# RWKV5 attention and a SoLU feed-forward block on one core: where rows are centred, how the float64 weights become float32, in which order the first iterations run

## The chip, the core and the metric

The kernel runs on one core of a Trainium2 chip. The metric is the device time of one execution in microseconds (us), as the median of several runs. The engines are TensorE (PE; its weight loads are listed as PEld), VectorE (DVE), ScalarE (ACT), GpSimd (POOL) and SyncE (SP, which here only issues DMAs). Each works through its own queue in order.

## The reference

```python
# r, k, v: (4, 8, 768, 48) float32; w, u: (8, 48)
for t in range(S):
    cur = einsum('bhd,bhe->bhde', u[None] * kt, vt)
    y[:, :, t] = einsum('bhd,bhde->bhe', rt, state + cur)
    state = w[None, :, :, None] * state + einsum('bhd,bhe->bhde', kt, vt)
x = y.transpose(0, 2, 1, 3).reshape(3072, 384)
h = x @ w_in                                  # (384, 1024)
e = exp(h - max(h));  solu = h * e / (sum(e) + 1e-9)
ln = (solu - mean(solu)) / sqrt(var(solu) + 1e-6) * g_ln
out = ln @ w_out                              # (1024, 384)
```

The two weight matrices reach the kernel as float64 words, since the setup divides float32 by a float64 root; r, k, v, w, u and g_ln are float32.

## The kernel before

The 3072 rows are 24 units of 128 tokens (a batch element and a chunk of 128 steps). A main loop runs `i` from -2 to 30. In iteration `i` it transposes r and k of unit `i + 2` (`turn_r`, `turn_k`), computes the decayed scores of unit `i + 1` (`scores`, tile `at`, masked into `AT` by VectorE's `copy_predicated`), the attention output of unit `i` (`finish`: `y_ps`, copied to `xT`, and the state update `kv_ps`), the input product of unit `j = i - 2` (`ffn_in`: `h_ps = xT·w_in`, then `Exp` on ScalarE), the unnormalised SoLU of unit `j` (`unit`: tile `solu` and its statistics), and the transposes and output product of unit `l = i - 7` (`turn_ln`: `t_ps`, copied to `lnT`; `ffn_out`: `o_ps`). So iterations 2 to 6 are early ones: they have an input product and no output product yet. From `i = 7` on both stand in each iteration, until units run out.

The order on each engine is the order in which the Python code issues instructions (`manual_schedule`); tiles of a pool wait for the release of the tile that held the buffer before. `psH` is one buffer of two PSUM banks for `h_ps`, `psM` four single banks for everything that is tagged "m". At most eight of SP's DMAs are under way at a time: each waits for the eighth before it.

`kp` (k times decay) and `rku` (r·k·u, of which VectorE's `own` is the sum per head and `diagonal` the product with the identity on ScalarE) are made by GpSimd three units ahead.

Weights are converted in 14 pieces: 6 of `w_in` (128x512 words of 8 bytes) and 8 of `w_out` (128x384). Per piece, `convert_a` takes on ScalarE the magnitude of the high word read as float32 (`mag`) and the scaled low word (`low`), `convert_b` on VectorE clamps `mag` and builds the float32 bits from high word and `mag` (L524, L528, L530), `convert_c` on GpSimd adds the low part, and for `w_out` `convert_d` multiplies by g on ScalarE. One piece each is converted at `i = -2` and `-1`, two each at `i = 0` to `5`; `w_in` is complete after `i = 1`.

Layer norm's mean is taken out of the weights: `column_sums` (L651) accumulates the column sums of the converted `w_out` in a PSUM bank over iterations 3 to 6, `column_mean` makes them a mean on all partitions, and `centre` (L662) subtracts it from the eight blocks of `w_out`, four on VectorE and four on GpSimd, at the end of iteration 6. The variance then comes from the sum and the sum of squares of a row:

```python
nc.scalar.activation(out=X["e"], in_=solu, func=ACT.Square, accum_out=ss)
nc.gpsimd.tensor_mul(sqm, tot, tot)
nc.gpsimd.tensor_scalar(out=sqm, in0=sqm, scalar1=-1.0 / dff ** 2, scalar2=1e-6, ...)
nc.gpsimd.tensor_scalar(out=var, in0=ss, scalar1=1.0 / dff, scalar2=sqm, ...)
```

At the end `check_sums` tests the row sums and the decays; a flag then decides at run time whether a second, general path (`general_path`, unchanged) runs. It does not run on these inputs.

Of the kernel before, what the change touches and what calls it, by code (L numbers as in the profile page):

```python
# [9 lines left out]
F32 = mybir.dt.float32  # L10
# [386 lines left out]
def direct_path(  # L397
# [101 lines left out]

    def load_weights(j):  # L500
        dst, src, _ = pieces[j]
        raws[j] = wpool.tile([128, dst.shape[1], 2], U32, tag="raw", name="raw", bufs=5)
        nc.sync.dma_start(out=raws[j].rearrange("p n o -> p (n o)"), in_=src)


# [2 lines left out]
    def convert_a(j):  # L508
        raw = raws.pop(j)
        n = raw.shape[1]  # L510
        lo, hi = raw[:, :, 0], raw[:, :, 1]
        mag = wpool.tile([128, n], F32, tag="mag", name="mag", bufs=3)
# [4 lines left out]
        step[j] = hi, mag, low  # L517

    def convert_b(j):
        hi, mag, low = step[j]  # L520
        ma = wpool.tile([128, mag.shape[1]], U32, tag="ma", name="ma", bufs=4)
# [19 lines left out]
    def convert_d(j):  # L541
        dst, _, f = pieces[j]
        ma, low = step.pop(j)
        if f is not None:
            nc.scalar.activation(out=dst, in_=ma.bitcast(F32), func=ACT.Copy,
                                 scale=g_sb[:, f : f + 1])


    load(0, "kr")
    load_weights(0)  # L550
    load(1, "kr")
    load(0, "v")
    load_weights(1)
    load(1, "v")
    load_weights(2)
    load(2, "kr")
    load_weights(3)
    load(2, "v")
    load_weights(4)
    load(3)  # L560

    ident = const.tile([128, 128], F32, name="ident")
    make_identity(nc, ident)
# [61 lines left out]

    def check_sums():

        good = small.tile([128, N], F32, name="good", bufs=1)
        good2 = small.tile([128, N], F32, name="good2", bufs=1)
        low = small.tile([128, 1], F32, name="low", bufs=1)  # L630
        nc.vector.tensor_single_scalar(out=good, in_=sums, scalar=1.0 / MOST, op=ALU.is_ge)
        nc.vector.tensor_single_scalar(out=good2, in_=sums, scalar=MOST, op=ALU.is_le)
        nc.vector.tensor_mul(good, good, good2)
        nc.vector.tensor_reduce(out=low, in_=good, axis=AX.X, op=ALU.min)
        n_ps = psM.tile([1, 1], F32, tag="m", name="n_ps")
        nc.tensor.matmul(n_ps, low, part[:, 0:1], start=True, stop=True)
        nc.vector.tensor_scalar(out=bad, in0=n_ps, scalar1=all_ok, scalar2=127.5 / 32,
                                op0=ALU.mult, op1=ALU.is_lt)

    part = const.tile([128, 128], F32, name="part")
    mean_sb = const.tile([128, dm], F32, name="mean_sb")
    nc.gpsimd.memset(part, 1.0 / 32)
    mean = []

    def column_sums(fs):
        if fs and not mean:
            mean.append(psM.tile([128, dm], F32, tag="m", name="mean_ps"))
        for f in fs:  # L650
            nc.tensor.matmul(mean[0][ts(f % 4, 32), :], part[:, 0:32], w_out_sb[:, f, :],  # L651
                             start=(f < 4), stop=(f >= KF - 4), skip_group_check=True)
        if KF - 1 in fs:
            nc.scalar.copy(out=mean_sb, in_=mean[0])

    def column_mean():
        ps = psM.tile([128, dm], F32, tag="m", name="mean_ps2")
        nc.tensor.matmul(ps, part, mean_sb, start=True, stop=True)
        nc.scalar.activation(out=mean_sb, in_=ps, func=ACT.Copy, scale=32.0 / dff)  # L659

    def centre(f, engine):
        engine.tensor_sub(w_out_sb[:, f, :], w_out_sb[:, f, :], mean_sb)  # L662

    live = {}

# [107 lines left out]

    def ffn_in(i):
        X = live[i]
        h_ps = psH.tile([128, dff], F32, name="h_ps")
        for n in range(dff // NX):
            for j in range(KD):
                nc.tensor.matmul(h_ps[:, ts(n, NX)], X["xT"][:, j, :], w_in_sb[:, j, ts(n, NX)],  # L779
                                 start=(j == 0), stop=(j == KD - 1))  # L780
        e = X["e"] = fpool.tile([128, dff], F32, name="e")
        nc.scalar.activation(out=e, in_=h_ps, func=ACT.Exp, accum_out=sums[:, i : i + 1])  # L782
        X["h"] = h_ps

    def unit(i):
        X = live[i]
        st = small.tile([128, 8], F32, name="st", bufs=LO + 3)
        rs, tot, ss, sqm, var, rstd = (st[:, n : n + 1] for n in range(6))
# [12 lines left out]
        X["rstd"] = rstd  # L801
# [23 lines left out]
        nc.sync.dma_start(out=out[ds(b * S + c * T, T), :], in_=o)  # L825


    ahead = 5
    todo = list(range(len(pieces)))
    conversions = {-2: 1, -1: 1, 0: 2, 1: 2, 2: 2, 3: 2, 4: 2, 5: 2}  # L830
    now = []
    decay_k(0)
    for i in range(-2, N + LA + LO):
        j, l = i - LA, i - LA - LO
        if i == 0:
            nc.sync.dma_start(out=g_sb, in_=moe_g_ln.rearrange("(c p) -> p c", p=128))
        if 0 <= i and i + 4 < N:
            load(i + 4)
        if i + 2 < N:
# [5 lines left out]
        fs = [pieces[p][2] for p in now if pieces[p][2] is not None]  # L845
        for p in now:
            convert_d(p)
        now = [todo.pop(0) for _ in range(conversions.get(i, 0))]
        for n, p in enumerate(now):
            convert_a(p)  # L850
            if n == 0 or i < LA:
                convert_b(p)
            if ahead < len(pieces):
                load_weights(ahead)
                ahead += 1
        if i + 3 < N:
            decay_k(i + 3)
            if i < 0:
# [4 lines left out]
            weigh(i + 3, nc.gpsimd)  # L863
        if i == 10:
            check_range()
        if 0 <= l and not i > N + LA - 1:
            turn_ln(l)
        if 0 <= j < N:
            ffn_in(j)
        column_sums(fs)  # L870
        if i + 2 < N and l >= 0:
            diagonal(i + 2)
        if 0 <= l and 0 <= j < N:
            unit(j)
        if i >= N + LA - 1 and l + 1 < N:
            turn_ln(l + 1)
        if l == N - 1:
            check_sums()
        if 0 <= l:
            ffn_out(l)  # L880
        if 0 <= i + 1 < N:
            scores(i + 1)
        if 0 <= j < N and l < 0:
            unit(j)
        if i < 0:
            diagonal(i + 2)
        if 0 <= i < N:
            finish(i)
        if l < 0 <= i:
# [4 lines left out]
        if KF - 1 in fs:  # L894
# [46 lines left out]
```

## Time and profile before

| what | us |
|---|---|
| median of three runs (lowest to highest) | 409.42 (406.99 to 409.58) |
| the profiled execution | 408.44 |
| its span, first to last instruction | 406.7 |
| PE busy in the span | 379.9 (93%) |
| ACT, DVE, POOL busy | 182.9, 164.5, 147.3 |

The profiled execution took 1.74 us more than its span, which lies outside the instructions. PE's busy share is an average over a start that waits much and a long middle that waits little, so it is read by stage. The chain of waits names, step by step from the last instruction backwards, what the next step waited for.

### The profile page before, as it was taken

Reading aid. Unit: us, or ns where it says so; the run is one execution under the profiler, and the core shown is the slowest. Engines: PE = TensorE matmul, PEld = TensorE weight load, DVE = VectorE, ACT = ScalarE, POOL = GpSimd, SP = SyncE. Lnnn points to the kernel's source line nnn. Section 1 sums busy time; section 2 is a strip of 40 time slices with the busy share of each in tenths; the row PEclk is TensorE's granted clock in tenths of the full one; section 3 lists DMA queues with packets and bytes.
Section 4 is the critical chain, followed back from the end, with each engine's and each line's share of the span. In section 5 each row is a group of like instructions: output and inputs, shape, how many; then the busy total and the mean of one; then the engine's idle time right before and its main releaser. Section 6 shows DMA issues by size and latency. Waiting matters only on the chain.

```text
span 406.7 us, 8991 instructions
## 1 busy us (share of the span) xinstructions
PE 379.9 (93%) x3737; PEld 238.2 (59%) x3737; DVE 164.5 (40%) x324; ACT 182.9 (45%) x428; POOL 147.3 (36%) x233
## 2 busy tenths in 40 slices
PE   2679989888999999999999999999999999999994
PEld 1566455554756756756756756756756665556662
DVE  6998766636413443513513513513513222012110
ACT  3875687753543542542542543543543433223210
POOL 4877666658324324324324324324320110011000
PEclk9867999998999999999999999999999999999998
DMA  8999896100404304404404403404000000000101
GB/s 166 274 204 256 148 176 104 21 2 2 80 1 79 79 2 79 79 1 79 79 2 80 79 0 79 81 0 79 21 2 19 21 22 1 21 19 21 39 19 48
DMA packets 81600, 26.04 MB, mean 64 GB/s; under 512 B 76557, under 2 KB 79758, under 8 KB 81550
## 3 DMA queue, kind: packets, MB, share of 16 engines
q1 hardware_dynamic: 81406, 25.18, 30.3%
q8 instruction: 31, 0.51, 0.6%
q10 hardware_dynamic: 144, 0.20, 0.2%
q14 instruction: 19, 0.16, 0.1%
HBM read 20.65 MB, written 4.72 MB: 62 GB/s over the span
## 4 chain that ended last, share of the span: by engine, by line
PE 82%; DVE 7%; ACT 4%; POOL 2%; DMA 2%; issue 2%; ACTq 0%; POOLq 0%; DVEq 0%
PE o_ps L821 31%; PE h_ps L779 28%; PE y_ps L744 7%; PE t_ps L810 5%; PE at L716 5%; PE tk_ps L704 2%; PE tr_ps L696 2%; ACT AT L690 2%; DVE AT L719 1%; DVE ma L530 1%; DVE solu L791 1%; DMA kpad<-in_k_dram 1%; PE kv_ps L762 1%; DVE ma L528 1%; POOL rku L679 1%
## 5 line engine op out<-in xcount | busy, mean ns | idle before, releaser
L779 PE MATMUL h_ps<-w_in_sb,xT 128*128 128x512 f32 x288 | 129.6, 600 | 1.0 <-DVE solu L791 1.0
L821 PE MATMUL o_ps<-w_out_sb,lnT 128*128 128x384 f32 x384 | 128.0, 487 | 0.0
L821 PEld LDWEIGHTS o_ps<-w_out_sb,lnT 128*128 128x128 f32 x384 | 72.4, 190 | 53.5 <-issue 8.1
L779 PEld LDWEIGHTS h_ps<-w_in_sb,xT 128*128 128x128 f32 x288 | 53.7, 193 | 59.8 <-issue 58.6
L782 ACT ACTIVATE e<-h_ps 128x1024 f32<-128x1024 f32 x24 | 24.5, 1023 | 92.3 <-PE h_ps L779 92.3
L719 DVE COPY_PREDICATED AT<-later,at 128x512 f32<-128x512 uint32 x48 | 32.8, 740 | 63.6 <-PE at L716 63.5
L690 ACT ACTIVATE AT<-ident,own 128x128 f32<-128x128 f32 x192 | 58.5, 388 | 0.0
L795 POOL TENSOR_TENSOR st<-st 128x1 f32<-128x1 f32 x24 | 4.6, 193 | 125.5 <-DVE solu L791 125.5
L789 DVE RECIPROCAL st<-sums 128x1 f32<-128x1 f32 x24 | 3.9, 161 | 101.6 <-ACT e L782 101.6
L793 ACT ACTIVATE e<-solu 128x1024 f32<-128x1024 f32 x24 | 25.1, 1047 | 21.1 <-DVE solu L791 21.1
L673 POOL TENSOR_TENSOR kp<-kpad,kdec 128x512 f32<-128x512 f32 x24 | 31.5, 1316 | 7.1 <-ACT kdec L601 5.2
L716 PEld LDWEIGHTS at<-rT,kT 48*64 48x64 f32 x768 | 23.0, 142 | 16.4 <-issue 11.5
L716 PE MATMUL at<-rT,kT 48*64 48x128 f32 (+1 forms) x768 | 29.6, 270 | 3.0 <-DVE AT L719 1.7
L824 ACT ACTIVATE o<-o_ps,st 128x384 f32<-128x384 f32 x24 | 13.9, 580 | 39.9 <-PE o_ps L821 16.9
L791 DVE SCALAR_TENSOR_TENSOR solu<-h_ps,st,e 128x1024 f32<-128x1024 f32 x24 | 30.8, 1284 | 2.5 <-DVE st L789 0.5
L769 POOL TENSOR_TENSOR state<-state,pw 64x192 f32<-64x192 f32 x32 | 16.1, 502 | 41.7 <-DVE state L768 40.5
L756 ACT COPY xT<-y_ps 128x384 f32<-128x384 f32 x24 | 11.4, 475 | 39.2 <-PE y_ps L744 39.2
L812 DVE COPY lnT<-t_ps 128x512 f32<-128x512 f32 x24 | 16.4, 684 | 28.6 <-PE t_ps L810 28.6
L810 PE MATMUL t_ps<-ident,solu 128*128 128x128 f32 x192 | 25.3, 274 | 2.3 <-ACT mean_sb L659 2.1
L744 PE MATMUL y_ps<-AT,vt 128*32 128x128 f32 x768 | 27.2, 285 | 0.0
L810 PEld LDWEIGHTS t_ps<-ident,solu 128*128 128x128 f32 x192 | 21.7, 141 | 5.5 <-ACT mean_sb L659 2.3
L680 POOL TENSOR_TENSOR rku<-rku,rpad 128x384 f32<-128x384 f32 x23 | 23.3, 1015 | 1.8
(80 smaller groups left out, 364.1 us busy)
## 6 DMA issues: line engine op xcount, KB each, us to landing
kpad<-in_k_dram SPq DMA_DIRECT2D x24, 192.0 KB, 4.0
rpad<-in_r_dram SPq DMA_DIRECT2D x24, 192.0 KB, 4.5
vt<-in_v_dram SPq DMA_DIRECT2D x24, 192.0 KB, 4.6
out_dram<-o SPq DMA_DIRECT2D x24, 192.0 KB, 2.0
raw<-in_moe_w_in_dram SPq DMA_DIRECT2D x6, 512.0 KB, 6.0
raw<-in_moe_w_out_dram SPq DMA_DIRECT2D x8, 384.0 KB, 4.6
u_bc<-in_u_dram ACTq DMA_DIRECT2D x1, 192.0 KB, 3.8
wq<-in_w_dram SPq DMA_DIRECT2D x1, 1.5 KB
```

What stands on the lines that cost most here:

```text
L673: nc.gpsimd.tensor_mul(X["kp"].rearrange("p h d -> p (h d)"), kpads[i % NLD].rearrange("p h d -> p (h d)"), kdec.rearrange("p a d -> p (a ...
L680: engine.tensor_mul(rku, rku, rpads[i % NLD][:, :, 0:D])
L690: nc.scalar.activation(out=AT[:, h, :], in_=ident, func=ACT.Copy, scale=X["own"][:, h])
L716: nc.tensor.matmul(pss[q][ts(c, P), a, c * P :], X["kT"][rows, a, ts(c, P)], X["rT"][rows, a, c * P :], start=True, stop=True)
L719: nc.vector.copy_predicated(A4[:, :, q, :], later.to_broadcast([128, HP, T]), pss[q])
L744: nc.tensor.matmul(y_ps[32 * g : 32 * g + 32, j, :], lhsT, rhs, start=(g not in opened), stop=stop, skip_group_check=True)
L779: nc.tensor.matmul(h_ps[:, ts(n, NX)], X["xT"][:, j, :], w_in_sb[:, j, ts(n, NX)], start=(j == 0), stop=(j == KD - 1))
L782: nc.scalar.activation(out=e, in_=h_ps, func=ACT.Exp, accum_out=sums[:, i : i + 1])
L791: nc.vector.scalar_tensor_tensor(out=solu, in0=X["h"], scalar=rs, in1=X["e"], op0=ALU.mult, op1=ALU.mult, accum_out=tot)
L793: nc.scalar.activation(out=X["e"], in_=solu, func=ACT.Square, accum_out=ss)
L810: nc.tensor.transpose(t_ps[:, f, :], X["solu"][:, ts(4 * g + f, 128)], ident)
L821: nc.tensor.matmul(o_ps, X["lnT"][:, f, :], w_out_sb[:, f, :], start=(f == 0), stop=(f == KF - 1))
```

## The change

There are six edits.

1. Rows are centred instead of weights. After `solu`, ScalarE replaces each row by `tot - 1024·solu` (`Identity` with scale and bias, in place), and `Square` follows it; the sign goes into `minus_g`. `column_sums`, `column_mean` and `centre` are gone, and two small GpSimd instructions per unit.
2. Weight words are converted without magnitude and clamp: `convert_a` has one ScalarE instruction, `convert_b` two VectorE instructions; for `w_in` the intermediate lies in PSUM (`part`, in the buffer of `h_ps`).
3. A range check of the words follows later: from `i = 7` to `20` each iteration loads one weight piece again (6 of 512 KB, 8 of 384 KB), and in the next one `check_words` takes the magnitude with its sum on ScalarE and the least on VectorE, ahead of `turn_ln`. `check_sums` reads the results.
4. k, r and v are loaded in another order, with a fifth buffer for k and r and a sixth for raw words.
5. In the early iterations `ffn_in` stands ahead of `turn_r` and `turn_k`, and `unit` ahead of `scores`.
6. `convert_d` and `convert_a` come ahead of `turn_r`.

```diff
-    NLD, NV = 4, 6
+    NLD, NV = 5, 6
...
-        nc.scalar.activation(out=mag, in_=hi.bitcast(F32), func=ACT.Abs)
         nc.scalar.activation(out=low, in_=lo, func=ACT.Copy, scale=2.0 ** -29)
...
+        part = ma
+        if pieces[j][2] is None:
+            part = psH.tile([128, dff], F32, tag="h", name="part").bitcast(U32)[:, 0:n]
-        nc.vector.tensor_scalar(out=mag, in0=mag, scalar1=FLOOR, scalar2=CEIL,
-                                op0=ALU.max, op1=ALU.min)
-        nc.vector.tensor_scalar(out=ma, in0=mag.bitcast(U32), scalar1=3, scalar2=0x3FFFFFF8,
+        nc.vector.tensor_scalar(out=part, in0=hi, scalar1=3, scalar2=0x3FFFFFF8,
                                 op0=ALU.logical_shift_left, op1=ALU.bitwise_and)
-        nc.vector.scalar_tensor_tensor(out=ma, in0=hi, scalar=0xC0000000, in1=ma,
+        nc.vector.scalar_tensor_tensor(out=ma, in0=hi, scalar=0xC0000000, in1=part,
                                        op0=ALU.bitwise_and, op1=ALU.bitwise_or)
...
+    def check_words(j):
+        raw = raws.pop(j)
+        mag = wpool.tile([128, raw.shape[1]], F32, tag="mag", name="mag", bufs=2)
+        nc.scalar.activation(out=mag, in_=raw[:, :, 1].bitcast(F32), func=ACT.Abs,
+                             accum_out=total[:, j : j + 1])
+        nc.vector.tensor_reduce(out=least[:, j : j + 1], in_=mag, axis=AX.X, op=ALU.min)
...
+        nc.scalar.activation(out=solu, in_=solu, func=ACT.Identity, scale=-float(dff), bias=tot)
         nc.scalar.activation(out=X["e"], in_=solu, func=ACT.Square, accum_out=ss)
-        nc.gpsimd.tensor_mul(sqm, tot, tot)
-        nc.gpsimd.tensor_scalar(out=sqm, in0=sqm, scalar1=-1.0 / dff ** 2, scalar2=1e-6,
-                                op0=ALU.mult, op1=ALU.add)
-        nc.gpsimd.tensor_scalar(out=var, in0=ss, scalar1=1.0 / dff, scalar2=sqm,
+        nc.gpsimd.tensor_scalar(out=var, in0=ss, scalar1=1.0 / dff, scalar2=1e-6 * dff ** 2,
...
+        if early and i >= LA:
+            for p in now[:1]:
+                convert_b(p)
+            ffn_in(j)
         if i + 2 < N:
             turn_r(i + 2)
...
+        if 7 <= i < 7 + len(pieces):
+            load_weights(i - 7)
+        if 8 <= i < 8 + len(pieces):
+            check_words(i - 8)
...
+        elif i >= LA:
+            unit(j)
         if 0 <= i + 1 < N:
             scores(i + 1)
...
-        if KF - 1 in fs:
-            column_mean()
-            for f in range(KF):
-                centre(f, nc.vector if f % 2 == 0 else nc.gpsimd)
```

**The loads at the start.** SP's queue from the second DMA on, before; `raw` is a weight piece, the number in `kpad`, `rpad`, `vt` the unit:

```order
L466 DMA kpad0_88<-in_k_dram 128x8x48
L466 DMA rpad0_84<-in_r_dram 128x8x48
L503 DMA raw_121<-in_moe_w_in_dram 128x1024
L466 DMA kpad1_89<-in_k_dram 128x8x48
L466 DMA rpad1_85<-in_r_dram 128x8x48
L466 DMA vt0_92<-in_v_dram 128x8x48
L503 DMA raw_126<-in_moe_w_in_dram 128x1024
L466 DMA vt1_93<-in_v_dram 128x8x48
L503 DMA raw_129<-in_moe_w_in_dram 128x1024
L466 DMA kpad2_90<-in_k_dram 128x8x48
L466 DMA rpad2_86<-in_r_dram 128x8x48
L503 DMA raw_133<-in_moe_w_in_dram 128x1024
```

The same place in the changed kernel:

```order
L466 DMA kpad0_89<-in_k_dram 128x8x48
L466 DMA rpad0_84<-in_r_dram 128x8x48
L504 DMA raw_128<-in_moe_w_in_dram 128x1024
L466 DMA kpad1_90<-in_k_dram 128x8x48
L466 DMA rpad1_85<-in_r_dram 128x8x48
L504 DMA raw_132<-in_moe_w_in_dram 128x1024
L466 DMA kpad2_91<-in_k_dram 128x8x48
L466 DMA rpad2_86<-in_r_dram 128x8x48
L504 DMA raw_136<-in_moe_w_in_dram 128x1024
L504 DMA raw_138<-in_moe_w_in_dram 128x1024
L466 DMA vt0_94<-in_v_dram 128x8x48
L504 DMA raw_141<-in_moe_w_in_dram 128x1024
```

Both loads of v have moved back and k and r of unit 2 forward; then follow k and r of unit 3, the sixth weight piece, v of unit 1, k and r of unit 4, v of unit 2.

**VectorE in iteration 1**, where the last two pieces of `w_in` are converted. Before:

```order
L697 TENSOR_TENSOR rT_428<-tr_ps_429,tab_162 128x512
L684 TENSOR_REDUCE own_435<-rku_357 128x8
L524 TENSOR_SCALAR mag_444<-mag_444 128x512
L528 TENSOR_SCALAR ma_448<-mag_444 128x512
L530 SCALAR_TENSOR_TENSOR ma_448<-raw_136,ma_448 128x512
L524 TENSOR_SCALAR mag_454<-mag_454 128x512
L528 TENSOR_SCALAR ma_458<-mag_454 128x512
L530 SCALAR_TENSOR_TENSOR ma_458<-raw_237,ma_458 128x512
```

In the changed kernel:

```order
L692 TENSOR_TENSOR rT_436<-tr_ps_437,tab_172 128x512
L679 TENSOR_REDUCE own_443<-rku_357 128x8
L528 TENSOR_SCALAR part_453<-raw_141 128x512
L530 SCALAR_TENSOR_TENSOR ma_452<-raw_141,part_453 128x512
L528 TENSOR_SCALAR part_457<-raw_145 128x512
L530 SCALAR_TENSOR_TENSOR ma_456<-raw_145,part_457 128x512
```

Two instructions are gone and the intermediate has another place; the first input product now waits for the last of these rows, since `part` holds its PSUM buffer.

**PE from the end of iteration 3 into iteration 4**, before:

```order
L744 MATMUL y_ps<-AT,vt_95 32x128 x16
L762 MATMUL kv_ps<-vt_95,kp 32x48 x16
L696 MATMUL tr_ps<-ident,rpad_86 128x128 x4
L704 MATMUL tk_ps<-ident,kp 128x128 x4
L779 MATMUL h_ps<-w_in_sb,xT 128x512 x6
L651 MATMUL mean_ps<-w_out_sb,part 32x384 x2
```

In the changed kernel, PE at the same place, and then ScalarE from iteration 3's `Exp` on:

```order
L739 MATMUL y_ps<-AT,vt_97 32x128 x16
L757 MATMUL kv_ps<-vt_97,kp 32x48 x16
L774 MATMUL h_ps<-w_in_sb,xT 128x512 x6
L691 MATMUL tr_ps<-ident,rpad_85 128x128 x4
L699 MATMUL tk_ps<-ident,kp 128x128 x4
```

```order
L777 ACTIVATE e,sums<-h_ps 128x1024
L700 COPY kT<-tk_ps 128x512
L788 ACTIVATE solu<-solu,st 128x1024
L789 ACTIVATE e,st<-solu 128x1024
L751 COPY xT<-y_ps 128x384
L685 ACTIVATE AT<-ident,own 128x128 x8
```

The product has moved ahead of the transposes, and on ScalarE the copy of `kT`, for which `scores` waits, now stands behind `Exp`.

## Rows read from the trace of the kernel before

**Rows 1.** The page, part 2: PE's busy tenths in 40 slices.
```profile
PE   2679989888999999999999999999999999999994
```

**Rows 2.** Stages cut at the starts of input products: length, busy time, clock.
```profile
34.76:44.69 9.93, 8.96 (x118) 5.26 (x117) 8.83 (x17) 4.04 (x10) 7.27 (x8) 0.97 1.11 216
44.69:55.95 11.26, 9.60 (x120) 5.38 (x121) 8.06 (x19) 9.25 (x23) 7.57 (x12) 1.00 0.82 158
55.95:67.13 11.18, 10.16 (x147) 5.95 (x145) 7.04 (x16) 8.17 (x21) 6.80 (x9) 1.00 0.83 127
...
78.31:93.33 15.02, 12.34 (x157) 7.33 (x156) 5.90 (x13) 10.41 (x28) 9.13 (x15) 1.00 0.01 2
93.33:109.39 16.06, 16.06 (x158) 9.45 (x158) 9.15 (x14) 6.13 (x15) 9.44 (x12) 0.90 0.16 35
...
124.62:306.30 181.68, 181.68 (x1930) 115.17 (x1928) 65.45 (x122) 80.11 (x191) 64.84 (x107) 1.00 0.25 48
```

**Rows 3.** The chain of waits: start, length, engine and line, count.
```profile
92.24 0.38 ACT mean_sb L659
...
93.33 6.85 PE h_ps L779 x12
...
105.34 1.02 PE at L716 x24
106.36 1.67 PE y_ps L744 x56
108.36 0.59 PE tr_ps L696 x4
...
109.39 0.87 PE t_ps L810 x8
110.26 5.15 PE h_ps L779 x12
```

**Rows 4.** SP's timeline: start, length, queue, line, the load it issues.
```profile
3.05 1.34 SPq L503 DMA_DIRECT2D raw<-in_moe_w_in_dram  x1
...
15.61 0.58 SPq L503 DMA_DIRECT2D raw<-in_moe_w_in_dram  x1
```

**Rows 5.** DMA issues at 3.05 and 15.61 us: KB, us to landing.
```profile
raw<-in_moe_w_in_dram SPq DMA_DIRECT2D x1, 512.0 KB, 5.4
...
raw<-in_moe_w_in_dram SPq DMA_DIRECT2D x1, 512.0 KB, 6.1
```

**Rows 6.** VectorE's timeline, conversion of weight words: start, length.
```profile
17.18 1.40 DVE L528 TENSOR_SCALAR ma<-mag 128x512 uint32<-128x512 uint32 x1
18.61 1.38 DVE L530 SCALAR_TENSOR_TENSOR ma<-raw,ma 128x512 uint32<-128x512 uint32 x1
...
22.64 0.43 DVE L528 TENSOR_SCALAR ma<-mag 128x512 uint32<-128x512 uint32 x1
...
26.60 0.69 DVE L530 SCALAR_TENSOR_TENSOR ma<-raw,ma 128x512 uint32<-128x512 uint32 x1
```

**Rows 7.** Groups by line and form: busy, mean ns, idle before and releaser.
```profile
L673 POOL TENSOR_TENSOR kp<-kpad,kdec 128x512 f32<-128x512 f32 x24 | 31.5, 1316 | 7.1 <-ACT kdec L601 5.2 <-DMA kpad<-in_k_dram 0.9
L791 DVE SCALAR_TENSOR_TENSOR solu<-h_ps,st,e 128x1024 f32<-128x1024 f32 x24 | 30.8, 1284 | 2.5 <-DVE st L789 0.5
...
L793 ACT ACTIVATE e<-solu 128x1024 f32<-128x1024 f32 x24 | 25.1, 1047 | 21.1 <-DVE solu L791 21.1
L782 ACT ACTIVATE e<-h_ps 128x1024 f32<-128x1024 f32 x24 | 24.5, 1023 | 92.3 <-PE h_ps L779 92.3
L679 POOL TENSOR_TENSOR rku<-kpad,u_bc 128x384 f32<-128x384 f32 x23 | 23.6, 1025 | 0.0
...
L812 DVE COPY lnT<-t_ps 128x512 f32<-128x512 f32 x24 | 16.4, 684 | 28.6 <-PE t_ps L810 28.6
...
L705 ACT COPY kT<-tk_ps 128x512 f32<-128x512 f32 x24 | 13.9, 579 | 14.2 <-PE tk_ps L704 14.2
...
L538 POOL TENSOR_TENSOR w_in_sb<-ma,low 128x512 uint32<-128x512 uint32 x6 | 7.7, 1290 | 5.8 <-DVE ma L530 5.8
```

More of the change, by code (lines that the diff above doesn't have):

```diff
@@ L551, in direct_path @@
     load(1, "kr")
+    load_weights(1)
+    load(2, "kr")
+    load_weights(2)
+    load_weights(3)
     load(0, "v")
-    load_weights(1)
+    load_weights(4)
+    load(3, "kr")
+    load_weights(5)
     load(1, "v")
-    load_weights(2)
-    load(2, "kr")
-    load_weights(3)
+    load(4, "kr")
     load(2, "v")
-    load_weights(4)
-    load(3)
     ident = const.tile([128, 128], F32, name="ident")
@@ L626, in check_sums @@
     def check_sums():
-        good = small.tile([128, N], F32, name="good", bufs=1)
-        good2 = small.tile([128, N], F32, name="good2", bufs=1)
+        L = len(pieces)
+        good = small.tile([128, 2, N + L], F32, name="good", bufs=1)
         low = small.tile([128, 1], F32, name="low", bufs=1)
-        nc.vector.tensor_single_scalar(out=good, in_=sums, scalar=1.0 / MOST, op=ALU.is_ge)
-        nc.vector.tensor_single_scalar(out=good2, in_=sums, scalar=MOST, op=ALU.is_le)
-        nc.vector.tensor_mul(good, good, good2)
@@ L635, in check_sums @@
+        nc.vector.tensor_reduce(out=low, in_=good, axis=AX.XY, op=ALU.min)
         n_ps = psM.tile([1, 1], F32, tag="m", name="n_ps")
-        nc.tensor.matmul(n_ps, low, part[:, 0:1], start=True, stop=True)
-        nc.vector.tensor_scalar(out=bad, in0=n_ps, scalar1=all_ok, scalar2=127.5 / 32,
+        nc.tensor.matmul(n_ps, low, ones, start=True, stop=True)
+        nc.vector.tensor_scalar(out=bad, in0=n_ps, scalar1=all_ok, scalar2=127.5,
                                 op0=ALU.mult, op1=ALU.is_lt)
-    part = const.tile([128, 128], F32, name="part")
@@ L643, in direct_path @@
[L643 to L652, printed above, removed]
-        if KF - 1 in fs:
-            nc.scalar.copy(out=mean_sb, in_=mean[0])
@@ L656, in column_mean @@
[L656 to L662, printed above, removed]
+    ones = const.tile([128, 1], F32, name="ones")
+    nc.gpsimd.memset(ones, 1.0)
     live = {}
@@ L787, in unit @@
         st = small.tile([128, 8], F32, name="st", bufs=LO + 3)
-        rs, tot, ss, sqm, var, rstd = (st[:, n : n + 1] for n in range(6))
+        rs, tot, ss, var, rstd = (st[:, n : n + 1] for n in range(5))
         nc.vector.reciprocal(out=rs, in_=sums[:, i : i + 1])
@@ L825, in ffn_out @@
         nc.sync.dma_start(out=out[ds(b * S + c * T, T), :], in_=o)
-    ahead = 5
+    ahead = 6
     todo = list(range(len(pieces)))
@@ L834, in direct_path @@
         j, l = i - LA, i - LA - LO
+        early = l < 0
+        if i == -1:
+            nc.sync.dma_start(out=g_sb, in_=moe_g_ln.rearrange("(c p) -> p c", p=128))
         if i == 0:
-            nc.sync.dma_start(out=g_sb, in_=moe_g_ln.rearrange("(c p) -> p c", p=128))
-        if 0 <= i and i + 4 < N:
+            load(3, "v")
+            load(4, "v")
+        if 1 <= i and i + 4 < N:
             load(i + 4)
+        for p in now:
+            convert_d(p)
+        now = [todo.pop(0) for _ in range(conversions.get(i, 0))]
+        for p in now:
+            convert_a(p)
+            if ahead < len(pieces):
+                load_weights(ahead)
+                ahead += 1
+        if early and i >= LA:
+            for p in now[:1]:
+                convert_b(p)
+            ffn_in(j)
         if i + 2 < N:
@@ L844, in direct_path @@
             turn_k(i + 2)
[L845 to L851, printed above, removed]
+        if i < LA:
+            for p in now:
                 convert_b(p)
-            if ahead < len(pieces):
-                load_weights(ahead)
-                ahead += 1
+        if i == LA:
+            nc.vector.tensor_single_scalar(out=minus_g, in_=g_sb, scalar=-1.0, op=ALU.mult)
         if i + 3 < N:
@@ L865, in direct_path @@
             check_range()
[L866 to L873, printed above, removed]
-            unit(j)
[L875 to L880, printed above, removed]
+        if 7 <= i < 7 + len(pieces):
+            load_weights(i - 7)
+        if 8 <= i < 8 + len(pieces):
+            check_words(i - 8)
+        if not early:
+            if i < N + LA:
+                turn_ln(l)
+            if j < N:
+                ffn_in(j)
+            if i + 2 < N:
+                diagonal(i + 2)
+            if j < N:
+                unit(j)
+            if i >= N + LA - 1 and l + 1 < N:
+                turn_ln(l + 1)
+            if l == N - 1:
+                check_sums()
+            ffn_out(l)
+        elif i >= LA:
+            unit(j)
         if 0 <= i + 1 < N:
             scores(i + 1)
-        if 0 <= j < N and l < 0:
-            unit(j)
         if i < 0:
@@ L888, in direct_path @@
             finish(i)
-        if l < 0 <= i:
+        if early and 0 <= i:
             diagonal(i + 2)
```

24 lines of the change are left out of this document (15 added, 9 removed).

## The prediction

> **What bounds the kernel now.** I read PE's slices first [rows 1]: from the eleventh slice on nearly every digit is 9, and the digits below 8 are the first three and the one at the end. Then I cut the span at the starts of input products [rows 2]. From 124.62 to 306.30 us PE is busy 181.68 of 181.68 us: there nothing but PE's own work counts. In the chain of waits one such iteration reads [rows 3]: scores 1.02, attention output 1.67, state products 0.33 (from 108.03 to 108.36), transposes of r and k 1.03, of the SoLU rows 0.87, input product 5.15, and the output product, 5.16 of the same chain (110.26 + 5.15 = 115.41 us; the iteration takes 15.23). None of these changes. What can change lies before the first full iteration's product at 93.33 us: the first product starts at 34.76 us, and the five stages after it take 9.93, 11.26, 11.18, again 11.18 and 15.02 us [rows 2], where PE has 8.6 to 9.3 us of work in an early iteration (product 5.15 + transposes 1.03 + scores 1.02 + output 1.67, or 1.0 where no state exists yet + state products 0.33 = 9.2). The product at 93.33 us itself took 6.85 instead of 5.15 us [rows 3]: its stage shows a granted clock of 0.90 after a wait for the mean [rows 2, 3], that is 1.2 GHz for part of it, and 1.00 elsewhere. So 1.70 us of clock belong to the start as well, and the comparable end of the start is 93.33 + 1.70 = 95.03 us.
>
> **First product earlier.** It needs six pieces of w_in and a free PSUM buffer, which now hangs on the last conversion on VectorE in iteration 1. I follow the one chain that ends there. Loads first: the first piece is down at 3.05 + 5.4 = 8.45 us, the fifth at 15.61 + 6.1 = 21.71 us [rows 4, 5]; between them the order before moves 4288 - 896 = 3392 KB, that is 256 KB per us. In the new order k of unit 3 ends at 4096 KB and the sixth piece at 4800 KB: 8.45 + 3200 / 256 = 20.95 us and 23.7 us. Then GpSimd, in order: `kp` of unit 3 1.32, two additions of pieces at 1.29, two `rku` instructions at 1.02 [rows 7], sum 5.94: 26.9 us. Then VectorE: `own` and four conversion instructions, each at most 0.69 [rows 6]: 3.45, so the product starts at about 30.35 us, 4.4 earlier. PE has been idle before it by some 3 us, since its last work waits for v of unit 1 (4992 KB, 24.5 us) and needs under 3 us after that. I therefore charge the product the 1.70 us that the one at 93.33 us paid after its wait.
>
> The 0.69 is a choice. L528 and L530 took 1.40 and 1.38 us in one place and 0.43 and 0.69 in others [rows 6]; the long ones stood beside running GpSimd instructions. With the long times on all four, the start is 2.8 us later, 33.1 us; with 0.43 for L528 0.5 sooner. The Trainium skill (SBUF — State Buffer, § Who interferes with whom) says that a VectorE instruction with two SBUF inputs, or in its two-port mode, shares a port with GpSimd, and the second to start waits for the whole of the other; one SBUF input alone doesn't wait. The trace agrees as far as it goes, since nothing else separates 1.38 from 0.69. By that rule `part` in PSUM ends the waits of these instructions; and by VectorE: DVE Perf Modes, § Why PSUM operands drop a tier, it also costs L528 its fast mode, so 0.69 rather than 0.43. Without the rule the sum would be the one with 33.1 us.
>
> **The five early iterations.** With the product ahead of the transposes, these run while ScalarE does `Exp`. The loop is then: product 5.15, `Exp` 1.02 and reading its sum, about 0.2, `kT` behind it 0.58 [rows 7], hand-overs about 0.1, scores 1.02, output 1.67, state products 0.33: 10.05 us, and 9.35 where no state exists (units 2 and 3). Is another engine slower? ScalarE was busy 8.17 us in an early stage [rows 2]; with `Identity` (priced as `Square`, 1.05 [rows 7]) less two instructions of some 0.55 this is 8.1; add a wait of about 1.1 for `solu` (1.28 [rows 7] and small change, less `kT`) and it is 9.2, under 10.05. Hand-overs come on top, so for unit 3 I credit nothing under 10.05. GpSimd and VectorE had 6.8 and 7.0 us [rows 2] and lose work. The buffer that the product needs is free in time: `solu` ends some 2.9 us after `Exp` starts, the product follows 4.9 after it. The last early stage adds the transposes 1.03 and 0.87, as no mean and no `centre` stands in it: 11.95. Sum: 9.35 + 3 x 10.05 + 11.95 = 51.45, and 53.15 with the slow clock, against 58.57 + 1.70 = 60.27 before: 7.1 us. Bounds: by PE's work alone 3.2 us better; with the middle stages as long as before 3.4 worse.
>
> **From there to the end.** `Identity` puts 1.05 us per unit on ScalarE, the check for 14 iterations one instruction of at most about 0.85 more and on VectorE one reduction of about 0.7. ScalarE was busy 80.11 of 181.68 us [rows 2], 6.7 of an iteration's 15.23. Its `o` moves by under half a us, and its bank is wanted only after scores, output, state products and a transpose, over 3 us later. Behind the check in the queues of ScalarE and VectorE stand the copies to `lnT` (0.68 [rows 7]), for which the output product waits; they move by about 1.1 us and are covered by the 5.15 us input product between [rows 3]. If that cover went, it would be 1.1 us in each of 14 iterations. The loads, 384 or 512 KB in 15 us, are issued an iteration ahead. Cost: nothing. The end has one matmul and its small tests as before.
>
> **Sum.** 4.4 + 7.1 = 11.5 us. From the profiled execution (408.44, span 406.7) this gives 396.9 and a span of 395.2; that execution lies 0.98 under the median of 409.42, from which I predict 397.9.
>
> **Rivals.**
> *The early iterations stay as long as they were.* `kT` waits for `Exp`, and `Exp` for ScalarE's products and low words of the next pieces, which wait for GpSimd and VectorE. Then the three middle stages stay at 11.2: 3.4 us lost, 401.3. For it: ScalarE's order now has 9.2 of 10.05 us, little air. Against: GpSimd has 6.8 us of work.
> *The start does not move.* With slower loads (the 216 GB/s of the stage at 34.76 us [rows 2], 211 KB per us, bring k of unit 3 2.7 us later) and the port waits (2.8) the first product comes at 35.8 us: 403.4. For it: each is in the trace. Against: both must hold, and k of unit 3 is moved ahead of 384 KB of v.
> *The clock falls in each early iteration,* as PE now waits about 0.8 us in every one: five times 1.70, or 406.4, no change. Against: stages with idle PE time of 1.0 to 1.7 us show 1.00 [rows 2].
> *Slower: the range check stalls the output product.* Place: `check_words` in iterations 8 to 21, with `lnT` behind it. It decides if a reloaded piece lands later than the input product's start plus some 4 us; then each us costs 14, and over 1.4 us per iteration makes the kernel slower by more than 1% (397.9 + 19.6 = 417.5 at 1.4). Against: 15 us from issue to use, where a piece landed in 6.1 us [rows 5].
> *The change does not do what it says:* the new range check trips on these weights, and the general path runs as well; with the two products alone, 24 x 10.3 us, that is over 640 us. Words of this size lie far inside its limits.
>
> **Chances.** Forecast 0.60 (395 to 400.5); long early iterations 0.17; start not moved 0.10; both of these 0.05 (406.8); clock 0.03; stall 0.04; flag 0.01. The range is 394.5 to 405: below, the bound by PE's work, above, each of the first two rivals with what the three runs differ (406.99 to 409.58). About 1% is what a measurement of this kernel can tell from no change. Faster by over 1% (under 405.3): 0.84; within 1%: 0.11; slower: 0.05.
>
> **What would show it.** First product at 30 us with a clock below 1.00; product starts then at 41.4, 51.5, 61.5, 71.6 and 83.5; PE's wait before scores put down to ScalarE's `kT`, 0.7 us in each early iteration; no wait for a mean; L530 at 0.69 throughout for `w_in`; from there iterations of 15.23 us. Wrong would be a first product after 33 us, early stages over 10.6, or PE waiting for `lnT` after 100 us.

## The result, and the profile after

The changed kernel takes 396.71 us (median of 4 runs, 396.06 to 397.32), the kernel before 409.43 (406.99 to 409.58): ratio 0.970, 95% interval 0.967 to 0.974. Its profiled execution took 396.06 us, with a span of 394.3; predicted were 397.9, 396.9 and 395.2. Three executions of 625.97, 986.6 (both of `scale_behind_exp` below) and 1800.76 us (the kernel before) are left out of the comparisons, and what disturbed them is open.

PE's slices of after, to be read beside [rows 1]: the third slice is 5, and from the fourth on all are 9 but the ninth (8) and the last (5). So most of PE's waiting now lies ahead of the first product, which starts at 30.49 us.

```profile
PE   2859999989999999999999999999999999999995
```

Stages of after, cut at the starts of input products (length, busy time of PE, PEld, DVE, ACT, POOL, granted clock), which answer to [rows 2]. The last row is the first full iteration.

```profile
30.49:41.49 11.00, 11.00 (x117) 6.22 (x117) 6.47 (x13) 2.35 (x6) 6.96 (x7) 0.78 1.06 242
41.49:51.02 9.53, 8.63 (x117) 5.27 (x117) 6.21 (x14) 8.41 (x20) 6.72 (x8) 1.00 1.27 211
51.02:60.53 9.51, 9.29 (x140) 5.92 (x141) 6.21 (x14) 8.38 (x20) 6.23 (x7) 1.00 0.99 145
60.53:70.36 9.83, 9.29 (x141) 5.93 (x141) 6.21 (x14) 8.51 (x20) 7.23 (x10) 1.00 0.32 63
70.36:82.94 12.58, 11.40 (x157) 7.84 (x158) 8.66 (x18) 11.30 (x26) 7.49 (x13) 1.00 0.21 59
82.94:98.18 15.24, 15.24 (x166) 9.73 (x165) 4.89 (x10) 9.57 (x24) 5.64 (x9) 1.00 0.21 43
```

The chain of waits of after (start, length, engine and line, count), which answers to [rows 3]: the end of the start, one early iteration, the way that the next early iteration takes instead, and the first full product.

```profile
26.07 1.02 POOL rku L675
...
29.75 0.70 DVE ma L530
...
30.49 7.75 PE h_ps L774 x12
...
50.91 1.16 ACT solu L788
...
52.09 1.15 ACT e L789 x2
53.23 0.36 ACT xT L751
53.60 2.34 ACT AT L685 x8
55.94 1.01 ACT w_out_sb L545 x2
56.96 0.91 ACT low L515 x2
57.86 1.00 ACT e L777 x2
...
59.09 1.30 DVE solu L786 x2
...
61.60 1.16 ACT e L789 x2
...
62.83 0.47 POOL st L790
...
63.39 0.54 POOL st L792
63.93 0.55 POOL state L764
...
65.14 1.01 POOL ma L538
...
66.17 0.62 ACT w_out_sb L545
...
82.94 5.15 PE h_ps L774 x12
```

The first product starts at 30.49 us and takes 7.75, 2.60 over the 5.15 of a product at the full clock; its stage has a granted clock of 0.78. The first full iteration's product starts at 82.94 us and takes 5.15. Against the comparable end of the start before, 95.03 us, that is 12.1 us earlier, and the spans differ by 406.7 - 394.3 = 12.4. So the time came from the start, as the prediction said. The two numbers are not quite the same thing: a later iteration gives 0.6 us back (`no_range_check` below), so ScalarE's last instruction starts 11.5 us earlier (389.92 instead of 401.41), and the other 0.9 us lie behind it, up to the end of the span, where nothing in the chain explains them.

A ring is here a chain of waits that comes back to its own start one iteration later; the longest ring sets the length of the iteration. The ring in the middle is not the predicted one: it goes round on ScalarE (row centring, squares, `xT`, diagonal, scaling of finished pieces, low words, `Exp`) and VectorE's `solu`. In the stages that start at 60.53 and 70.36 us the chain takes a second way: from ScalarE's squares over GpSimd (statistics, state, the addition of a piece) back to ScalarE's scaling. PE is in neither, and `kT` (L700) does not appear.

### The profile page after: what moved, and what is told of

Read it like the earlier page. It is cut to its first block, busy times and chain, and to the rows that moved or that the text cites. A ratio compares the mean times of both kernels' runs of the same rounds, so it can differ in the third digit from the quotient of the medians.

```text
span 394.3 us, 8911 instructions
## 1 busy us (share of the span) xinstructions
PE 372.2 (94%) x3719; PEld 235.0 (60%) x3719; DVE 159.0 (40%) x324; ACT 208.1 (53%) x464; POOL 129.4 (33%) x181
## 4 chain that ended last, share of the span: by engine, by line
PE 79%; ACT 7%; DVE 6%; POOL 3%; issue 1%; DMA 1%; SPq 0%; POOLq 0%; ACTq 0%; DVEq 0%
PE o_ps L813 32%; PE h_ps L774 25%; PE y_ps L739 7%; PE t_ps L802 5%; PE at L711 4%; PE tr_ps L691 2%; DVE solu L786 2%; PE tk_ps L699 2%; ACT solu L788 1%; ACT e L789 1%; ACT AT L685 1%; PE kv_ps L757 1%; ACT e L777 1%; POOL w_in_sb L538 1%; ACT w_out_sb L545 1%
## 5 line engine op out<-in xcount | busy, mean ns | idle before, releaser
L790 POOL TENSOR_SCALAR st<-st 128x1 f32<-128x1 f32 x24 | 5.6, 235 | 183.0 <-ACT e L789 183.0
L668 POOL TENSOR_TENSOR kp<-kpad,kdec 128x512 f32<-128x512 f32 x24 | 30.8, 1284 | 11.2 <-DMA kpad<-in_k_dram 5.1
L788 ACT ACTIVATE solu<-solu,st 128x1024 f32<-128x1024 f32 x24 | 27.4, 1141 | 12.4 <-DVE solu L786 12.4
L711 PE MATMUL at<-rT,kT 48*64 48x64 f32 (+1 forms) x768 | 28.1, 262 | 0.0
L711 PEld LDWEIGHTS at<-rT,kT 48*64 48x64 f32 x768 | 21.8, 137 | 10.5 <-issue 10.2
L751 ACT COPY xT<-y_ps 128x384 f32<-128x384 f32 x24 | 11.4, 474 | 31.4 <-PE y_ps L739 31.4
L739 PE MATMUL y_ps<-AT,vt 128*32 128x128 f32 x768 | 26.3, 279 | 0.9 <-DMA vt<-in_v_dram 0.9
```

Of the source, the lines that this page charges most:

```text
L668: nc.gpsimd.tensor_mul(X["kp"].rearrange("p h d -> p (h d)"), kpads[i % NLD].rearrange("p h d -> p (h d)"), kdec.rearrange("p a d -> p (a ...
L711: nc.tensor.matmul(pss[q][ts(c, P), a, c * P :], X["kT"][rows, a, ts(c, P)], X["rT"][rows, a, c * P :], start=True, stop=True)
L739: nc.tensor.matmul(y_ps[32 * g : 32 * g + 32, j, :], lhsT, rhs, start=(g not in opened), stop=stop, skip_group_check=True)
L788: nc.scalar.activation(out=solu, in_=solu, func=ACT.Identity, scale=-float(dff), bias=tot)
```

## The experiments

All are edits of the changed kernel. The product starts, five early ones and the first full one, are from PE's timeline (which lists the last some 0.16 us ahead of the chain). "First" is the length of the first product, from 5.3 to 8.5 us with its clock; so the stages are best compared by "rest", the time from the second start to the last. Of the ratios only those of `order_and_centred`, `clamp_back` and `best` stand clear of that of after; the other intervals overlap it, and there the differences are read from the trace of one execution each.

| kernel | product starts, us | first | rest | median, us | ratio to before (95%) |
|---|---|---|---|---|---|
| before | 34.76 44.69 55.95 67.13 78.31 93.17 | 5.57 | 48.48 | | 1 |
| after | 30.49 41.49 51.02 60.53 70.36 82.78 | 7.75 | 41.29 | 396.71 | 0.970 (0.967 to 0.974) |
| old_load_order | 32.41 43.60 53.13 62.64 72.48 84.90 | 7.45 | 41.30 | 398.18 | 0.973 (0.969 to 0.977) |
| part_in_sbuf | 29.22 41.04 51.30 60.80 70.63 83.04 |  | 42.00 | 395.65 | 0.968 (0.964 to 0.971) |
| old_early_order | 30.32 41.48 51.51 61.51 71.53 82.75 | 7.11 | 41.27 | 395.69 | 0.968 (0.963 to 0.972) |
| weights_centred | 30.50 41.99 51.35 61.37 71.39 84.94 | 8.31 | 42.95 | 398.50 | 0.975 (0.971 to 0.978) |
| order_and_centred | 30.57 40.10 51.85 63.09 74.33 89.18 | 5.42 | 49.08 | 404.95 | 0.989 (0.984 to 0.995) |
| clamp_back | 32.92 43.57 54.06 64.55 75.42 87.97 | 6.83 | 44.40 | 401.64 | 0.983 (0.979 to 0.987) |
| no_range_check | 30.38 40.81 50.33 59.85 69.68 82.10 | 7.09 | 41.29 | 396.33 | 0.972 (0.969 to 0.974) |
| kt_late | 30.30 41.22 51.21 61.21 71.21 84.36 | 7.06 | 43.14 | 397.58 | 0.974 (0.971 to 0.977) |
| diagonal_on_vector | 30.37 42.28 51.91 61.55 71.70 84.50 | 8.46 | 42.22 | 397.37 | 0.973 (0.970 to 0.976) |
| scale_behind_exp | 30.35 40.71 49.27 58.52 67.77 79.92 | 7.11 | 39.21 | 393.28 to 395.70 | 0.967 (0.963 to 0.971) |
| warm_start | 34.00 42.72 52.23 61.75 71.59 84.00 | 5.31 | 41.28 | 398.13 | 0.975 (0.973 to 0.978) |
| best | 30.94 39.50 48.06 57.31 66.56 78.71 | 5.31 | 39.21 | 391.62 | 0.958 (0.955 to 0.961) |

### One part undone

**old_load_order**: `load(0, "v")`, `load(1, "v")`, `load(2, "v")` go back ahead of the loads that the first product needs.

> The changed kernel with the loads ahead of the loop in their old order (buffers as changed). My account of the first product: it hangs on k of unit 3 through GpSimd (in the changed kernel GpSimd waited 1.30 us for that k, until 21.26 us). In the old order k of unit 3 ends at 4480 instead of 4096 KB, 1.5 us later at 256 KB per us: first product at about 32.0 us, time about 398.2 us. Rival: the first product hangs on the conversions alone and the order of the loads gives nothing: 30.5 us and 396.7 us.

Measured: 32.41 us, 398.18 us. GpSimd's timeline has `kp` of unit 3 behind its wait for that k (in brackets), here and, in the second fence, in after:

```profile
23.19 1.27 POOL L668 TENSOR_TENSOR kp<-kpad,kdec 128x512 f32<-128x512 f32 x1 [1.91 <-DMA kpad<-in_k_dram]
```

```profile
21.26 1.28 POOL L668 TENSOR_TENSOR kp<-kpad,kdec 128x512 f32<-128x512 f32 x1 [1.30 <-DMA kpad<-in_k_dram]
```

So k of unit 3 held up GpSimd, as expected, by 1.9 us where 1.5 were forecast. The chain of waits names r of unit 3 at this place, but GpSimd's additions start 1.23 us behind `kp` in both kernels (24.42 and 22.49 us), so r cost nothing. The order of the loads is worth 1.9 us at the first product and nothing after it. The added buffers of the fourth edit were not undone by themselves.

**part_in_sbuf**:

```diff
-        if pieces[j][2] is None:
-            part = psH.tile([128, dff], F32, tag="h", name="part").bitcast(U32)[:, 0:n]
```

> The changed kernel with the first conversion instruction of w_in writing into its SBUF tile, as for w_out, and not into PSUM. Port account: L528 and L530 wait for running GpSimd instructions again, up to 0.7 us each on the last four: first product between 31.5 and 33.3 us, time 397.7 to 399.5 us, and single L528 or L530 records of w_in above 1.0 us. Rival, the times of 1.40 and 1.38 us had another cause: 0.43 and 0.69 us throughout, first product at 30.0 us, time 396.2 us.

VectorE's timeline (start, length; the two-input conversion is L528 in this kernel), and PE's, with the wait in brackets:

```profile
23.89 1.65 DVE L528 SCALAR_TENSOR_TENSOR ma<-raw,ma 128x512 uint32<-128x512 uint32 x1
...
31.62 1.65 DVE L528 SCALAR_TENSOR_TENSOR ma<-raw,ma 128x512 uint32<-128x512 uint32 x1
```

```profile
29.22 4.68 PE L772 MATMUL h_ps<-w_in_sb,xT 128*128 128x512 f32 x10
34.75 1.13 PE L772 MATMUL h_ps<-w_in_sb,xT 128*128 128x512 f32 x2 [0.85 <-POOL w_in_sb L536]
```

The port account was right on the instruction: 1.65 us against 0.69 in PSUM, and the last conversion ends at 33.2 instead of 30.45 us. It was wrong on the path. Borrowing the product's PSUM bank is itself a wait: without it ten of the product's twelve records run from 29.22 us, while the last two pieces are still being converted, and only the last two wait for the end of that. The earlier start is lost again: the chain of waits runs from the late conversions through VectorE's queue to the first `solu`, and the second product starts at 41.04 us after a wait of 1.92 us and takes 7.08 instead of 5.39. The intervals of the two ratios overlap: no difference is shown.

**old_early_order**: `turn_r`, `turn_k` ahead of `convert_d`, `convert_a` and `ffn_in`, and `unit` behind `scores`, as before.

> The changed kernel with the early iterations in their old order: transposes ahead of the input product, SoLU behind the scores. If the order is what shortened the stages: VectorE takes the scores' two copies (1.35 us) ahead of the product of the SoLU, so ScalarE's row centring starts some 1.5 us later, and the middle stages go from 9.5 to 11.0 or 11.2 us: time 400.5 to 401.7 us. Rival, ScalarE's busy time alone sets the stages: it is the same in both orders, 9.5 to 9.8 us, time 396.7 us.

Neither holds: the stages are 10.03, 10.00 and 10.02 us, up to half a us longer, but the last early one is 11.4 in place of 12.6, and the product at 82.75 us stands where it stood. Alone, the new order is worth nothing that can be measured.

**weights_centred**: `column_sums`, `column_mean`, `centre` and the old statistics are back, `Identity` is out.

> The changed kernel with w_out centred by its column means as before, and no centring of rows. The mean returns in the stage before the first full iteration: that stage 15.0 instead of 12.6 us and its product 6.85 instead of 5.15 us, 4.1 us together; ScalarE loses 1.15 us in each early stage, so the waits for the SoLU (0.90, 0.22 and 0.54 us) go: 396.7 + 4.1 - 1.7 = 399.1 us. Rival A: the mean is hidden by the new order: 395 us. Rival B, ScalarE does not limit the early stages: they stay at 9.5 to 9.8 us, 400.8 us.

Measured 398.50 us. The middle stages no longer wait for `solu`: 10.02 us, all of it PE's work with 0.77 for the column sums. The last early stage takes 13.55 us, and its product 5.3: the slow clock of [rows 3] is not there. So the row centring alone is worth 1.7 us of "rest", less than expected. That 399.1 us came near is luck: the mean costs less than the 4.1 us forecast, and the middle stages grow where they were to shrink.

**order_and_centred**: the two edits together.

> The changed kernel with both: w_out centred by its means as before, and the early iterations in their old order. Alone, the old order gave back 0.0 us at the first full iteration's product and the centring 2.2 us, and neither showed a slow product there. If the two interact, and the new order is what lets the mean hide: the stage before the first full iteration is near the 15.02 us of before and its product near 6.85 us, 4.5 us or more given back together, 401 us or more. Rival, they only add: 2.2 us given back, product of 5.3 us, 398.5 us.

They interact: 404.95 us. The rest is 7.8 us longer, where the sum of both alone is 1.6, and the product at 89.18 us takes 7.01, 1.7 too much. The middle stages are 11.24 us, with the clamp gone. The chain of waits, one iteration:

```profile
63.26 5.15 PE h_ps L796 x12
68.41 0.77 PE mean_ps L668 x4
69.18 1.10 PE at L733 x20
...
70.98 0.73 DVE AT L736
...
71.78 1.29 DVE solu L808 x2
73.07 0.26 DVE state L785
...
73.36 0.37 DVE state L785
...
73.87 0.63 PE tk_ps L721 x4
74.50 5.15 PE h_ps L796 x12
```

PE's transposes of k, ahead of the product in the old order, wait for VectorE's `state`, 1.08 us in its timeline. `state` empties `kv_ps`, and it stands behind the two copies and `solu` in VectorE's queue. In `old_early_order` this wait is absent. An early iteration takes four tiles of the four-buffer pool (`tr_ps`, `tk_ps`, `y_ps`, `kv_ps`), and the mean's accumulator, held from iteration 3 to 6, is a fifth, so I read the wait as the missing fourth buffer; that reading rests on the program, not on a run with a fifth buffer. The kernel before shows the same ring in its chain, with the clamp, in the stages of 11.18 us of [rows 2]:

```profile
64.57 1.29 DVE solu L791 x2
65.86 0.26 DVE state L768
...
66.67 0.63 PE tk_ps L704 x4
67.29 5.15 PE h_ps L779 x12
```

**clamp_back**: `Abs` on ScalarE and `max`/`min` on VectorE are back in `convert_a` and `convert_b`.

> The changed kernel with the clamp of the weight words back: ScalarE's Abs and VectorE's clamp for each of the 14 pieces (the later range check stays). Undone one by one, load order, row centring, early order and PSUM gave back 2.1, 2.1, 0 and 0 of the 12.1 us by which the first full iteration's product came earlier. If the missing 7.5 us are the clamp: first product at 32 to 33 us, middle stages 1.1 us longer each (two Abs of some 0.55 us ahead of Exp), 403 to 404 us. Rival, the parts overlap and the clamp alone also gives back only some 2 us (first product 1.4 us later, stages as they are): 398.5 us.

Between the two, and clear of after by its ratio: 401.64 us, the first product 2.4 us later, then stages of 10.49, 10.49 and 10.87 us, the rest 3.1 us longer. In the chain `Abs` (0.45), the clamp (0.37) and the two conversions stand between ScalarE's scaling and VectorE's `solu`.

**no_range_check**: no second load, `check_words` or its tests.

> The changed kernel without the later range check of the weight words: no second load, no Abs with sum, no minimum. My account: nothing of it is on the path, 396.4 to 397.0 us; the longer stage at 128.90 us (15.78 us) stays, as it comes from the small load of w in iteration 10. Rival, ScalarE, VectorE or the loads are held up by it: over 1 us less, under 395.7 us.

396.33 us, the intervals overlap. Only one iteration differs: by PE's timeline it takes 16.03 us in after (128.49 to 144.52), 15.43 here, and 15.24 elsewhere. So the check costs 0.6 us once, which my account had put down to the load of `w` alone; the other 0.2 stand there without the check as well, and in the kernel before (15.45), with the load and its tests on VectorE.

### What sets the early iterations

**kt_late**:

```diff
-            turn_k(i + 2)
+            held = turn_k(i + 2, early and i >= LA)
...
             diagonal(i + 2)
+        if early and i >= LA:
+            held()
```

> The changed kernel with ScalarE's copy to kT, in the early iterations, behind row centring, squares, xT and diagonal instead of right behind Exp. As the prediction put it, the scores wait for this copy: it would come some 6 us later and lengthen each early iteration by about as much, over 415 us. By the trace of the changed kernel the scores use the kT of the iteration before, and ScalarE's own chain sets the stages: the copy leaves a gap where ScalarE waits for the SoLU anyway and adds about 0.5 us to each of four stages, 398.2 to 398.9 us, with no wait before scores.

397.58 us, stages of 9.99, 10.00, 10.00 and 13.15 us, the rest 1.85 us longer. The list of waits has no scores:

```profile
PE h_ps L775 <- DVE solu L787: 3.4, 4, 1.4
```

So scores do not wait for this copy; ScalarE's ring got longer by this copy, 0.47 us. The prediction's loop falls, and with it the remark under the change that `scores` waits for the copy of `kT` behind `Exp`: scores use the `kT` of the iteration before.

**diagonal_on_vector**: `tensor_scalar` by `own` on VectorE in place of ScalarE's eight products.

> The changed kernel with the eight diagonal products of each early iteration (2.35 us on ScalarE) on VectorE. ScalarE's chain account: PE's waits of 0.90, 0.22, 0.54 and 1.18 us in the early stages go, the middle stages come down to PE's own 9.3 us: 396.7 - 2.8 = 393.9 us. Rival, something else (kT, GpSimd's products, VectorE) sets them: stages stay at 9.5 to 9.8 us or grow by the 1.5 us that VectorE gets, 396.7 us or more.

The rival holds. The stages stay or grow a little (9.63, 9.64, 10.15), and with them falls "ScalarE's own time sets them". ScalarE's timeline shows what took the place of the 2.35 us:

```profile
54.40 0.61 ACT L545 ACTIVATE w_out_sb<-ma,minus_g 128x384 f32<-128x384 f32 x1
57.34 0.62 ACT L545 ACTIVATE w_out_sb<-ma,minus_g 128x384 f32<-128x384 f32 x1 [2.33 <-POOL ma L538]
57.87 1.01 ACT L515 ACTIVATE low<-raw 128x384 uint32<-128x384 uint32 x2
58.76 1.03 ACT L781 ACTIVATE e<-h_ps 128x1024 f32<-128x1024 f32 x1
```

The second piece's addition on GpSimd stands behind the unit's statistics, which wait for `Square`; ScalarE's scaling waits for the addition, and `Exp` stands behind the scaling. In after, in the stage from 60.53 us, this second ring ends 0.20 us behind the first.

**scale_behind_exp**:

```diff
-        for p in now:
+        done = now
+        for p in done if i < LA else []:
             convert_d(p)
...
             turn_k(i + 2)
+        for p in done if i >= LA else []:
+            convert_d(p)
```

> The changed kernel with ScalarE's scaling of the two finished pieces of w_out (1.01 us in each early iteration from the second on), which stands ahead of Exp and waits for GpSimd's addition, put behind Exp and the copy to kT. With the diagonal on VectorE the stages stayed, and the chain then ran from ScalarE's squares over GpSimd's statistics, state and addition to this scaling and so to the next Exp. If the early stages are set by two chains of nearly the same length that both pass through this scaling ahead of Exp: both are cut, the scaling falls into ScalarE's wait for the SoLU (1.09 us), middle stages at PE's 9.3 us, no wait of t_ps for xT: 396.7 - 2.8 = 393.9 us. Rival, a third chain (VectorE's SoLU behind its conversions, or kT) is as long: 396.7 us.

Both rings are cut. The chain of waits has PE alone in the middle stages:

```profile
49.34 5.35 PE h_ps L774 x12
54.69 0.44 PE tr_ps L691 x4
55.12 0.44 PE tk_ps L699 x4
55.56 1.02 PE at L711 x24
56.58 1.67 PE y_ps L739 x56
58.25 0.34 PE kv_ps L757 x32
58.59 5.35 PE h_ps L774 x12
```

8.56, 9.25 and 9.25 us per stage, the rest 2.1 us shorter; of the 2.8 expected, `t_ps` keeps 0.89 in its wait for `xT`. So what the prediction told as its first rival, `Exp` behind ScalarE's products that wait for GpSimd, is at work in after, at 0.3 to 1.0 us per stage. The four executions lie at 393.28 to 395.70 us, and the interval of their ratio still overlaps that of after; `best` below, which holds this edit, is clear of it.

### The clock of the first product, and the sum

**warm_start**:

```diff
+            if i == LA:
+                warm_ps = psM.tile([128, HP, T], F32, tag="m", name="warm_ps")
+                for _ in range(8):
+                    nc.tensor.matmul(warm_ps, ident, back, start=True, stop=True)
             ffn_in(j)
```

> The changed kernel with eight matmuls more, 128x512 as in the product and read by nothing, in PE's queue between the last state products of the start and the first input product, where PE waits 3.7 us. If the first product's 7.75 us come from the lowered clock after this wait: the eight run in 3.4 us at the full clock, the product starts at 30.5 us as before and takes 5.15 us: 394.1 us. Rival, the product is slow by its operands or by other engines' work beside it: 7.75 us again, 396.7 us; or the eight run at half the clock and push the product back by up to 3 us, 397 to 400 us.

I had taken one matmul for 0.43 us; it is 0.89, two records each. So the eight pushed the product back:

```profile
27.03 7.13 PE L849 MATMUL warm_ps<-tab,ident 128*128 128x512 f32 x16
34.00 5.31 PE L774 MATMUL h_ps<-w_in_sb,xT 128*128 128x512 f32 x12
```

But the product took 5.31 us, so the 2.4 us over are the clock's: over the product the granted clock is 1.00 here, 0.69 in after. Started 3.5 us later, it ended only 1.1 us later. Its later place beside other work is not the reason: in `best` it starts at 30.94 us and takes 5.31 as well. Four kernels without these matmuls also had a granted clock of 1.00 from 16 to 26.5 us (`old_load_order`, `weights_centred`, `kt_late`, `diagonal_on_vector`), waited, and had 0.64 to 0.76 over the product.

**best**: `scale_behind_exp`, four such matmuls, and the load of `wrow` in iteration 0.

> The changed kernel with three edits: the scaling behind Exp and kT, four matmuls of 0.86 us that nothing reads in PE's wait before the first product (the eight took 7.13 us and let the product take 5.31 us), and the small load of w in iteration 0 in place of 10. If the three add: -2.8, -2.4 (the first product 5.3 in place of 7.75 us) and -0.5 us (the longer stage at 128.90 us), 391.0 us. Rival, the early stages take up what the first product gives, as the next product then waits for the SoLU: 393.4 us.

391.62 us, ratio 0.958. The first product starts 0.45 us later, takes 5.31, and the next starts at 39.50 with no wait: the gains add, 2.0 us up to the second start and 2.1 in the rest. The early load of `wrow` brought little: that iteration takes 15.75 us by PE's timeline, since its four instructions on VectorE still stand ahead of the copy to `lnT`.

## Why the prediction was right, and where it was not

**First product: right.** Predicted 30.35 us, measured 30.49. The chain is the predicted one: GpSimd's `kp` at 21.26 (k down at 20.95 predicted), its last `rku` to 27.09 (26.9), then `own` and four conversions at 0.69 to 0.70. The choice of 0.69 was by the rule of the Trainium skill (SBUF — State Buffer, § Who interferes with whom), and `part_in_sbuf` agrees with it: 1.65 us with two SBUF inputs, where GpSimd's `kp` also took 1.45 instead of 1.28. The runner-up, long times on all four and a product at 33.1 us, did not occur. `part_in_sbuf` does not stand for it: there the conversions end at 33.2 us, but only one of the last four is that long (1.01, 0.69, 0.42 and 1.65), they begin 1.9 us later, and the product does not wait for them. The load order (1.9 us) and the clamp (2.4) carried this term.

**Slow clock: mis-sized.** Charged 1.70 us, measured 2.60 (7.75 - 5.15); `warm_start` and `best` show that it is the clock. The first stage as a whole came out by luck, 11.00 us against 9.35 + 1.70 = 11.05: what the clock took beyond the charge, the rest of the stage gave back (3.25 us behind the product, where 4.20 were counted).

**Early iterations: the sum near by luck, the step wrong.** 53.15 us predicted with the slow clock, 52.45 measured (82.94 - 30.49), in which the middle stages are 1.3 us shorter than counted and the last one 0.6 longer. The failed step is "`kT` behind it 0.58 ... scores 1.02": scores use the `kT` of the iteration before, and `kt_late` shows that they wait for nothing of it. In its place two rings run through ScalarE's scaling ahead of `Exp`, at 9.5 to 9.8 us; I had priced ScalarE at 9.2 and dropped it "under 10.05". The prediction also never asked why the stages before took 11.18 us. `order_and_centred` shows it: the old order together with the mean. Neither alone makes them so long (10.0 us each), and the clamp is not needed for it (11.24 without it); either edit breaks that ring. Once broken, the clamp matters, 1.0 us per stage. So what the parts give back alone (loads 1.9, clamp 2.4 + 3.1, centring 1.7, order 0) sums to 9.1 us, and with the pair (7.8 + 1.7) to 16.9, while 12.1 was gained: the limits lie over one another. The bound by PE's work alone, 3.2 us under the 51.45 counted, was too tight: `best` takes 47.77 us (78.71 - 30.94), 3.7 under it.

**Mean and `centre`: right.** No wait for a mean, no slow product at 82.94 us; the last early stage 12.58 against 11.95, as `t_ps` waits 1.18 us for `xT` behind ScalarE's centring.

**Steady part: nothing, but for 0.8 us.** Iterations take 15.24 us, as predicted. `Identity` took 1.14 us, not 1.05, and is hidden. One iteration takes 16.03: SP issues `wrow` at 128.26 behind the other loads, four VectorE instructions on it and the `least` of the range check then stand ahead of `lnT`, and the output product waits 0.5 us. It is the place of the stall rival, once and not in 14 iterations; `no_range_check` removes 0.6. The other rivals did not occur.

**Sum.** 11.5 us predicted, 12.4 in span and 12.7 in medians. By parts the span has 4.3 (first product), 7.8 (early iterations with the clock, 7.1 predicted), 0.6 lost in one later iteration, and 0.9 behind the last instruction, which nothing here explains: from ScalarE's last instruction to the end of the span it is 4.7 us before and 3.8 in after, and 5.0 in `no_range_check`, whose last output is the same.

## What to carry to other kernels

Before costing a change to a loop, name the ring that sets its length now, from the chain of waits, and then ask which ring is next: here a ring of 11.2 us hid one of 10.5, that one of 9.5 to 9.8, and that PE's 9.25. An instruction that waits for another engine's late work should not stand in a queue ahead of one that others wait for; moving two scalings behind `Exp` was worth 2.1 us by the product starts, while moving 2.35 us of work to another engine was worth nothing. A part undone alone gives its worth beside the other parts only, so undo pairs as well.

## What the runs showed that was not expected

The first product took 5.42 us after a wait of 1.47 us (`order_and_centred`) and 7.11 after one of 1.48 (`old_early_order`); after waits of 3.5 to 4.6 us it took 6.83 to 8.46. Later products differ in the same way: 5.39 us after a wait of 1.86 (`clamp_back`, the product at 54.06 us) and 7.08 after one of 1.92 (`part_in_sbuf`, at 41.04). So the length of the wait alone does not decide it; what else does is open. Four matmuls that nothing reads, 3.70 us, brought the first product to 5.31.

VectorE's test of one row, 1x384, took 1.14 us in after (L636), its twin ahead of it 0.40 (L635). GpSimd's `rku` (0.99 us) ran beside the long one; no run here separates the cause.
